# A planned order: the offsets of its due times put in a table with three phases

## The chip, the cores and the metric

One core of one Trainium2 chip. The time is that of the device for one execution, in microseconds (us). The core has TensorE (PE) for matmuls, VectorE (DVE), ScalarE (ACT) and GpSimd (POOL) for elementwise work, and SyncE (SP), which issues most of the DMAs. Each engine works through a queue of its own that is written when the kernel is built.

## The reference

Attention with random features feeds a two-layer network. 8 batches, 8 heads, 576 positions, head size 64, 128 features; the network has 4608 tokens, width 512, inner width 2048. All of it is float32.

```python
def phi(x):                                   # x is q or k, scaled by D ** -0.25
    h = einsum('bhsd,md->bhsm', x, omega) - sum(x * x) / 2
    return exp(h - max(h)) / sqrt(m)
kv = einsum('bhsm,bhsd->bhmd', phi(k), v)
z = sum(phi(k), axis=2)
x = einsum('bhsm,bhmd->bhsd', phi(q), kv) / (einsum('bhsm,bhm->bhs', phi(q), z) + 1e-6)
h = x.transpose(0, 2, 1, 3).reshape(4608, 512) @ w_in
out = (maximum(h, 0) + log1p(exp(-abs(h)))) @ w_out
```

## The kernel before

**Precision.** The layers' products are made of three matmuls each on operands split into a high part in a fast format and a rest: high x high, high x rest, rest x high. This is why every matmul line of a layer comes in threes (L923 to L925 for layer 1, written to `h`; L952 to L954 for layer 2, written to `acc`). The weights come as 64-bit words and are turned into such pairs in the first part of the kernel (`plan_weights`, lines L274 to L303).

**Attention.** Four heads of a batch are a quad; there are two quads in each of the 8 batches. A unit is one or two position tiles of keys or of queries of a quad (`plan_unit`). It loads a tile `xk` or `xq`, takes squares and norms, projects it, takes maxima over the features and the exponent. Keys and the first batches' queries are projected in one pass (`project`, L399); queries of later batches and some tails are split first (`spq`, L413 and L417) and projected with `product` (L424). A key tile gives its buffer back with its second maxima, a split tile with its norms. Key units are added up for z (`add`) and, when all five tiles are there, multiplied with v in a `burst` (L563, L664). Queries are divided by the denominators (`den`, L785), transposed on DVE (`flip`, L816), sent to DRAM and back in another order (`away`, L823; `back`, L839), and multiplied with kv (`num` in `plan_x`, L865). The result, split into high and rest, is the input of the layers. It lies in a ring of 1024 tokens.

**Layers.** Ten blocks of tokens (two of 256, then eight of 512) with 16 steps of the inner width each (`plan_step`): twelve matmuls of layer 1, three activations for the softplus on ACT, `plus`, `high` and `low` (the rest of the softplus, L946), then three matmuls of layer 2 for each 128 tokens. After 16 steps a block is copied out and stored.

**The order.** Nothing in it is a loop at run time. All work is first put down as `Work` items with a cost on each engine that may take it, a due time, what must be done before, and the buffers it takes and gives. `in_order` then plays the whole kernel through: it finds the engine on which the earliest item could start, takes of that engine's items that could start within `PATIENCE` of it the one with the lowest due time (less `GLUE` for half-array matmul groups behind another such group), and moves that engine's clock on by the item's cost. Items due more than `AHEAD` after the earliest unfinished one are left out. The outcome is one sequence, from which every engine's queue is written. At run time the queues hold to it, with semaphores where one needs the other. Costs are formulas: a load of n bytes is `max(0.55, n / 360e3)` us on SP, and its data count as there `DL` = 2.3 us later.

A due time is a base time plus an offset. The bases come from the place of the unit or step (`FIRST`, `NEXT`, `PACE` = 2.92 us for a step, `SPREAD`); the offset was a number written in each call, one for each kind of work:

```python
ld = do(
    "SP", dma(size), due - 2.45, load, behind=prev.get("load"),
    take=[("w" if early else "x", b, "x")], delay=DL, spare=2 if early else 0,
)
```

Of the buffers, there is one for the tiles of later batches (`"x": 1`), one for split tiles, three for features, two for `h`. Ahead of 70 us of the plan, `with_fill` puts filling matmuls (`fill`, L1104) where PE would have a gap.

Of the kernel before, what the change touches and what calls it, by code (L numbers as in the profile page):

```python
# [17 lines left out]
PSUM = bass.MemoryType.PSUM  # L18
# [3 lines left out]
D = 64  # L22
# [12 lines left out]
AHEAD = 211.97  # L35
MARGIN = 0.00
# [4 lines left out]
PATIENCE = {"PE": 0.00, "DVE": 0.00, "ACT": 0.17, "POOL": 0.00, "SP": 1.29}  # L41
LEAN = {"DVE": 0.22, "POOL": 0.14, "ACT": 0.00}
# [5 lines left out]
GLUE = 0.35  # L48
HOLD = 0.00
LATER = 4.74  # L50
EARLY_Q = 0.52
EARLY_T = 0.00

# [134 lines left out]
def favor_softplus_kernel(ctx, tc, q0, k0, qx, kx, tx, vv, om, wi, wo, out):  # L188
# [55 lines left out]
    def dma(size, n=1):  # L244
        return max(0.55 * n, size / 360e3)
# [19 lines left out]
    def plan_weights(nm, fc, due):  # L265

        src, w = (wi, w1) if nm == "i" else (wo, w2)
        last = fc == NFC - 1
# [33 lines left out]
        def low_part(e):  # L302
# [5 lines left out]
            "SP", 1.46, due + 8.41, load, delay=DL, spare=0 if last else 2,  # L308
# [3 lines left out]
        a = do(("ACT", "DVE"), (aw, dw2), due, low_bits, after=[l], port=True)  # L312
        b = do("ACT", aw, due, rebias, after=[l])
        c = do("DVE", dw, due, joined, after=[a, b], port=True)
        d = do(
            ("ACT", "DVE"), (aw, dw2), due, high_part, after=[c] + (in_w if last else []), take=[("w", box, "w")], port=True,
# [3 lines left out]
        return do(("DVE", "POOL"), (dw, pw), due, low_part, after=[d], give=[(box, "raw")], port=True)  # L320


    def plan_save(q, y, due, after):

        def save():
            c, t = slice(2 * q.qd, 2 * q.qd + 2), slice(q.b * D, (q.b + 1) * D)
            nc.sync.dma_start(rest[:, c, t], y["r"])

        saves.append(do("SP", 0.6, due, save, after=after, give=[(y, "rs")], delay=DL))
# [17 lines left out]
    def plan_unit(q, kind, us, due, early, other=None):  # L347

        u = us[0]
        nm = f"{kind}{q.nm}_{u}"  # L350
# [112 lines left out]
        def exponent(j):  # L463
# [9 lines left out]
            "SP", dma(size), due - 2.45, load, behind=prev.get("load"),  # L473
# [3 lines left out]
        s = do(("POOL", "ACT"), (pool(w), act(w)), due, squares, after=[ld])  # L477
# [3 lines left out]
        if q.b < SPLIT["t" if tail else kind]:  # L481
            r = do("DVE", dve(w), due + 18.07, norms, after=[s], behind=prev.get("norms"), take=sm)
            prev["norms"] = r
            p = do(
                "PE", 0.02 + 0.224 * nt, due - 25.82, project, after=[ld], mode="r",
# [9 lines left out]
            e = do("DVE", dve(n), due - 9.42, less_norms, after=[e], port=True)  # L495
            e = do("DVE", dve(n), due - 7.64, bias, after=[e], port=True)
            for j in range(2):
                give = [(b, ("ppb", j))]
                es.append(do(
                    "ACT", n // 2 * 0.25, due + 9.96, lambda j=j: exponent(j), after=[e], behind=es[0] if j else None,  # L500
                    give=give + ([(b, "sms")] if j else []),
                ))
        else:
            hs, ls, l = [], [], None
            for j in range(2):
                h = do(
                    ("ACT", "DVE"), (act(w) + 0.1, dve(w, 2) + 0.115), due + 0.00, lambda e, j=j: high(e, j), after=[ld], behind=hs[-1] if hs else None,
# [3 lines left out]
                l = do(("DVE", "POOL"), (dve(w) + 0.115, pool(w) + 0.05), due - 113.62, lambda e, j=j: low(e, j), after=[h], behind=l, port=True)  # L511
                ls.append(l)
            r = do("DVE", dve(w), due - 20.57, norms, after=[s] + ls, behind=prev.get("norms"), take=sm, give=[(b, "x")])
            prev["norms"] = r
            e, p = None, prev.get("product")
            for t in range(nt):
                p = do(
                    "PE", 0.236, due - 27.09, lambda t=t: product(t), after=ls, behind=p, take=[(kind_, b, ("ppb", t))],
# [3 lines left out]
                    ("ACT", "DVE"), (act(2 * M, PSUM), dve(2 * M)), due - 49.46, lambda e, t=t: first(e, t), after=[p], behind=e,  # L522
                    take=[] if t else phs,
                )
                e = do("DVE", dve(2 * M), due - 32.71, lambda t=t: second(t), after=[c], give=[(b, ("ppb", t))])
            prev["product"] = p
            e = do("DVE", dve(n * M) + 0.07 * (len(to) - 1), due + 72.38, all_maxima, after=[e, r])
            e = do("DVE", dve(n), due - 62.34, less_norms, after=[e], port=True)
            e = do("DVE", dve(n), due - 40.07, bias, after=[e], port=True)
            es = []  # L530
            for t in range(nt):
                es.append(do(
                    "ACT", 0.587, due - 48.11, lambda t=t: exponents(t), after=[e], behind=es[-1] if es else None,
# [15 lines left out]
    def plan_keys(q, us, due, b, es, early):  # L549
# [36 lines left out]
        def plan_turn(after, give=[]):  # L586
            old = quads[q.n - 2].nums if q.n >= 2 else []
            t = do("PE", 0.15, due - 17.12, turn, after=[after], take=[(any_, q.slots, "kv")], give=give)
            q.kvl = do(
                ("ACT", "DVE"), (act(2 * M, PSUM), dve(2 * M)), due - 5.81, turned, after=[t] + old,  # L590
# [4 lines left out]
        if early:  # L595
# [16 lines left out]
            def first_scaled():  # L612
# [4 lines left out]
                "PE", 0.97 if u < 4 else 0.5, due + 44.03, outer, after=es + [q.kvm], give=[(b, "x")],  # L617
                take=[("acc", q.slots, "kt")] if u == 0 else [],
            )
            if u == 4:  # L620
                q.kvl = do(
                    "ACT", act(4 * D + 4, PSUM), due - 27.00, first_scaled, after=[q.kvm], give=[(q.slots, "kt")],
# [4 lines left out]
        def add(e):  # L627
# [16 lines left out]
            ("POOL", "DVE"), (k * pool(w), k * dve(w)), due + 4.30, add, after=es + [q.sum],  # L644
# [29 lines left out]
        def in_z():  # L674
# [6 lines left out]
        ldv = do("SP", 1.8, due + 46.00, load_v, take=[("v", q.slots, "v")], delay=DL)  # L681
        q.kvm = do(
            "PE", 0.1 + 0.224 * 12, due - 54.75, burst, after=q.es + [ldv, q.sum], take=[(any_, q.slots, "kt")],
            give=[(x, "phs") for _, x in q.units] + [(q.slots, "v")], mode="c",
        )
        a = do("ACT", act(4 * M, PSUM), due + 43.95, lambda: scaled(4 * M), after=[q.kvm], give=[(q.slots, "kt")])
        t = plan_turn(a)
        r = do("SP", 0.55, due - 26.01, out_z, after=[a], delay=DL)
        q.zc = do(
            "SP", 0.73, due + 17.88, in_z, after=[r, t], take=[("zb", q.slots, "zb")], give=[(q.slots, "s")], delay=DL  # L690
        )

    def plan_first(q, u, due, b, es, nm):
# [51 lines left out]
        def x_low():  # L745
# [3 lines left out]
        t = do("PE", 0.13 * n, due - 142.98, turn, after=es, take=[("any", y, "tp")])  # L749
        h = do(("ACT", "DVE"), (act(n * M, PSUM), dve(n * M)), due - 126.19, turned, after=[t], give=[(y, "tp")])  # L750
        a = do(
            "PE", 0.9, due - 147.22, num, after=[h, q.kvl], take=[("any", y, "nb")], behind=q.nums[-1] if q.nums else None,
            give=[(q.slots, "zb")] if u == NU - 1 else [],
        )
        i = do("DVE", 0.25, due - 94.20, invert, after=[a], take=[("dn", y, "dns")], port=True)
        v = do("DVE", dve(4 * D), due - 35.90, divide, after=[i], give=[(y, "nb"), (y, "dns")])
        k = do("PE", 0.28, due - 15.07, back, after=[v], take=[("any", y, "xb")], give=[(b, "x")])
        q.nums.append(a)
        h = do(
            ("DVE", "ACT"), (dve(2 * w), act(2 * w, PSUM)), due + 25.84, x_high, after=[k], take=[("pt", y, "rs")] if u == 4 else [],  # L760
# [5 lines left out]
        l = do("DVE", dve(2 * w), due - 36.37, x_low, after=[h], give=[(y, "xb")])  # L766
# [3 lines left out]
    def plan_queries(q, u, due, bu, es, nm, first):  # L770
# [21 lines left out]
        def divide(e):  # L792
# [4 lines left out]
            "DVE", 1.7 if u < 4 else 1.3, due + 43.55, den, after=es + [q.zc], take=[("dn", b, "dns")],  # L797
            give=[(q.slots, "zb")] if u == NU - 1 else [], port=True,
        )
        d = do("DVE", 0.09, due - 60.76, invert, after=[d])  # L800
        return do(("POOL", "DVE"), (1.0 * f, dve(n * M)), due + 84.05, divide, after=[d], give=[(b, "dns")], port=True)
# [410 lines left out]
```

## Time and profile before

| | |
|---|---|
| three runs | 1013.47, 1015.00, 1015.49 us; median 1015.0 |
| span of the profiled execution | 1014.7 us |
| its mean granted TensorE clock | 0.998 |
| PE, PEld busy | 998.7, 808.7 us |
| DVE, ACT, POOL busy | 744.1, 659.4, 118.7 us |
| HBM | 85.68 MB read, 27.03 MB written |

The profile has no time of its own for the profiled execution beside its span; the span is 0.3 us under the median of the runs and inside their spread. PEld is the loading of weights into the array, which goes on beside the matmuls. Where a row says "idle before" or puts a wait in brackets, it names the engine and line that ended it.

### The profile page before, as it was taken

Reading aid. Unit: us, or ns where it says so; the run is one execution under the profiler, and the core shown is the slowest. Engines: PE = TensorE matmul, PEld = TensorE weight load, DVE = VectorE, ACT = ScalarE, POOL = GpSimd, SP = SyncE. Lnnn points to the kernel's source line nnn. Section 1 sums busy time; section 2 is a strip of 40 time slices with the busy share of each in tenths; the row PEclk is TensorE's granted clock in tenths of the full one; section 3 lists DMA queues with packets and bytes.
Section 4 is the critical chain, followed back from the end, with each engine's and each line's share of the span. In section 5 each row is a group of like instructions: output and inputs, shape, how many; then the busy total and the mean of one; then the engine's idle time right before and its main releaser. Section 6 shows DMA issues by size and latency. Waiting matters only on the chain.

```text
span 1014.7 us, 17024 instructions
## 1 busy us (share of the span) xinstructions
PE 998.7 (98%) x5752; PEld 808.7 (80%) x5752; DVE 744.1 (73%) x2027; ACT 659.4 (65%) x1592; POOL 118.7 (12%) x125
## 2 busy tenths in 40 slices
PE   9999999999999999999999999999999999999997
PEld 8788788877777787878787777778788778888886
DVE  6999988988888787878787887878797733223222
ACT  6999977766666675856576666656575644444443
POOL 2212221010021010110112011201011100000000
PEclk9999999999999999999999999999999999999999
DMA  9774354443442424343333433352433121001001
GB/s 350 300 274 165 115 151 126 151 114 94 125 141 69 139 80 145 115 130 94 118 127 102 113 96 111 95 146 73 138 129 89 42 79 63 1 1 42 1 1 42
DMA packets 64174, 113.81 MB, mean 112 GB/s; under 512 B 18236, under 2 KB 36824, under 8 KB 64088
## 3 DMA queue, kind: packets, MB, share of 16 engines
q1 hardware_dynamic: 63848, 112.34, 34.9%
q8 instruction: 46, 0.75, 0.3%
q10 hardware_dynamic: 240, 0.39, 0.1%
q14 instruction: 40, 0.33, 0.1%
HBM read 85.68 MB, written 27.03 MB: 111 GB/s over the span
## 4 chain that ended last, share of the span: by engine, by line
PE 80%; DMA 7%; DVE 6%; ACT 5%; issue 1%; SPq 0%; POOL 0%; DVEq 0%; POOLq 0%
PE acc L952 12%; PE h L923 12%; PE acc L953 11%; PE acc L954 11%; PE h L924 11%; PE h L925 11%; PE xp L865 3%; PE kt L563 2%; PE ppk L399 2%; PE ppq L424 2%; DMA xk<-kx 2%; DVE junk L785 2%; DMA xq<-q 1%; DMA xq<-qx 1%; DMA rawo<-wo 1%
## 5 line engine op out<-in xcount | busy, mean ns | idle before, releaser
L923 PE MATMUL h<-xh,wi 128*128 128x512 f32 (+1 forms) x640 | 239.6, 374 | 1.5 <-DVE u L938 1.4
L924 PE MATMUL h<-xl,wi 128*128 128x512 f32 (+1 forms) x640 | 236.0, 369 | 0.0
L925 PE MATMUL h<-xh,wi 128*128 128x512 f32 (+1 forms) x640 | 235.5, 368 | 0.0
L952 PE MATMUL acc<-wo,gh 128*128 128x512 f32 x576 | 231.1, 401 | 0.5 <-ACT kvs L581 0.5
L953 PE MATMUL acc<-wo,gh 128*128 128x512 f32 x576 | 225.4, 391 | 0.0
L954 PE MATMUL acc<-wo,gl 128*128 128x512 f32 x576 | 224.8, 390 | 0.0
L929 ACT ACTIVATE u<-h 128x512 f32<-128x512 f32 (+1 forms) x160 | 89.1, 558 | 168.8 <-PE h L925 161.6
L938 DVE SCALAR_TENSOR_TENSOR u<-h,u 128x512 f32<-128x512 f32 (+1 forms) x160 | 101.3, 633 | 119.4 <-ACT u L935 117.2
L923 PEld LDWEIGHTS h<-xh,wi 128*128 128x128 f32 x640 | 120.5, 188 | 30.0 <-issue 5.4
L925 PEld LDWEIGHTS h<-xh,wi 128*128 128x128 f32 x640 | 120.5, 188 | 20.5
L924 PEld LDWEIGHTS h<-xl,wi 128*128 128x128 f32 x640 | 120.6, 188 | 18.8
L952 PEld LDWEIGHTS acc<-wo,gh 128*128 128x128 f32 x576 | 108.1, 188 | 30.0 <-issue 7.2
L954 PEld LDWEIGHTS acc<-wo,gl 128*128 128x128 f32 x576 | 108.2, 188 | 24.0 <-DVE gl L946 0.4
L953 PEld LDWEIGHTS acc<-wo,gh 128*128 128x128 f32 x576 | 108.4, 188 | 17.9
L942 ACT CAST gh<-u 128x512 fp32r<-128x512 f32 (+1 forms) x122 | 71.4, 585 | 57.0 <-PE acc L953 56.0
L946 DVE TENSOR_TENSOR gl<-u,gh 128x512 fp32r<-128x512 f32 (+1 forms) x128 | 86.1, 673 | 27.8 <-ACT gh L942 25.9
L935 ACT ACTIVATE u<-u 128x512 f32<-128x512 f32 (+1 forms) x160 | 94.4, 590 | 4.8
L932 ACT ACTIVATE u<-u 128x512 f32<-128x512 f32 (+1 forms) x160 | 94.5, 591 | 3.9
L785 DVE CUSTOM_DVE_ANT_0 junk<-phq,zb 128x128 bf16<-128x128 f32 (+1 forms) x228 | 78.1, 342 | 17.3 <-ACT phq L446 1.4
L794 POOL TENSOR_TENSOR phq<-phq,dnq 128x512 f32<-128x512 f32 (+1 forms) x43 | 45.5, 1063 | 212.1 <-DVE dnq L790 114.2
L946 POOL TENSOR_TENSOR gl<-u,gh 128x512 fp32r<-128x512 f32 (+1 forms) x32 | 36.2, 1131 | 280.3 <-ACT gh L942 147.5
L469 ACT ACTIVATE phk<-ppk,smk 128x128 f32<-128x128 f32 x230 | 63.6, 376 | 3.5 <-DVE smk L461 2.1
(129 smaller groups left out, 1293.6 us busy)
## 6 DMA issues: line engine op xcount, KB each, us to landing
xk<-kx SPq DMA_DIRECT2D x28, 512.0 KB
xq<-qx SPq DMA_DIRECT2D x28, 512.0 KB
fdq<-flq SPq DMA_DIRECT2D x28, 512.0 KB
qq<-fdq SPq DMA_DIRECT2D x112, 128.0 KB
rawi<-wi SPq DMA_DIRECT2D x16, 512.0 KB
rawo<-wo SPq DMA_DIRECT2D x16, 512.0 KB
out<-o SPq DMA_DIRECT2D x32, 256.0 KB
v<-vv SPq DMA_DIRECT2D x14, 576.0 KB
```

The source lines that it names most:

```text
L785: nc.vector.tensor_tensor_reduce(jk[r, c % jk.shape[1]], ph[r, c], q.zb[r, h], 1.0, 1e-6, ALU.mult, ALU.add, dn[r, 0, c : c + 1])
L923: nc.tensor.matmul(b["h"], wh, xh[:, cc, t], start=cc == 0, stop=False)
L924: nc.tensor.matmul(b["h"], wh, xl[:, cc, t], start=False, stop=False)
L925: nc.tensor.matmul(b["h"], wl, xh[:, cc, t], start=False, stop=cc == NCC - 1)
L929: nc.scalar.activation(b["u"], b["h"], AF.Abs)
L932: nc.scalar.activation(b["u"], b["u"], AF.Exp, scale=-1.0)
L935: nc.scalar.activation(b["u"], b["u"], AF.Ln, bias=1.0)
L938: nc.vector.scalar_tensor_tensor(b["u"], b["h"], 0.0, b["u"], ALU.max, ALU.add)
L946: (nc.vector if e == "DVE" else nc.gpsimd).tensor_tensor(b["gl"], b["u"], b["gh"].bitcast(F32), ALU.subtract)
L952: nc.tensor.matmul(acc[tt], gh, w2[fc][:, 0], start=fc == 0, stop=False)
L953: nc.tensor.matmul(acc[tt], gh, w2[fc][:, 1], start=False, stop=False)
L954: nc.tensor.matmul(acc[tt], gl, w2[fc][:, 0], start=False, stop=fc == NFC - 1)
```

## The change

Every offset moves into a table, `DUE`, under the name of its kind of work, with three numbers: `by(key, due)` adds the one of the current phase. The phase is set on entry to three functions, from the weights' chunk, the unit's batch or the block. All but a few of the numbers in the table differ from those in the calls before. Besides, `AHEAD`, `GLUE` and some of `PATIENCE` and `LEAN` have other values. Costs, buffers, base times, the functions that emit instructions and `in_order` itself stay as they are.

```diff
-AHEAD = 211.97
+AHEAD = 223.0942
-PATIENCE = {"PE": 0.00, "DVE": 0.00, "ACT": 0.17, "POOL": 0.00, "SP": 1.29}
-LEAN = {"DVE": 0.22, "POOL": 0.14, "ACT": 0.00}
+PATIENCE = {"PE": 0.0164, "DVE": 0.00, "ACT": 0.1684, "POOL": 0.00, "SP": 1.1241}
+LEAN = {"DVE": 0.2277, "POOL": 0.0900, "ACT": 0.00}
-GLUE = 0.35
+GLUE = 0.9002
+PHASE = [0]
+def by(key, due):
+    return due + DUE[key][PHASE[0]]
+DUE = {
+    "weights.load": (9.28, -4.63, 1.37),
...
+    "weights.high_part": (-0.76, -4.04, -53.28),
...
+    "unit.load": (-1.26, -0.71, 5.53),
...
+    "unit.project": (-24.15, -41.49, -112.25),
+    "unit.maxima": (-2.46, -38.05, 0.88),
...
+    "unit.norms2": (-20.57, -20.57, -12.55),
+    "unit.product": (-27.09, -27.09, -98.56),
...
+    "unit.all_maxima": (72.38, 72.38, -55.22),
...
+    "queries.den": (43.55, 41.33, 97.91),
...
+    "flip.away": (-64.23, 73.34, -92.28),
...
+    "step.layer1": (39.90, -4.88, -5.74),
...
+    "step.low": (4.10, 86.96, -5.17),
+    "step.layer2": (62.69, 4.31, 4.11),
...
+    "step.store": (52.41, -38.32, 125.86),
...
+}
     def plan_weights(nm, fc, due):
+        PHASE[0] = 0 if fc < 5 else 1 if fc < 10 else 2
...
-            "SP", 1.46, due + 8.41, load, delay=DL, spare=0 if last else 2,
+            "SP", 1.46, by("weights.load", due), load, delay=DL, spare=0 if last else 2,
...
     def plan_unit(q, kind, us, due, early, other=None):
+        PHASE[0] = min(q.b, 2)
...
-            "SP", dma(size), due - 2.45, load, behind=prev.get("load"),
+            "SP", dma(size), by("unit.load", due), load, behind=prev.get("load"),
...
-                    "DVE", dve(n // 2 * M), due - 5.19, lambda j=j: maxima(j), after=[p, e], give=[(b, "x")] if j and not early else [],
+                    "DVE", dve(n // 2 * M), by("unit.maxima", due), lambda j=j: maxima(j), after=[p, e], give=[(b, "x")] if j and not early else [],
...
     def plan_step(i, t0, n, fc, due, acc, box):
+        PHASE[0] = 0 if i < 2 else 1 if i < 4 else 2
...
-                "PE", 0.70 if n < TB else 1.36, due, lambda ccs=ccs: layer1(ccs), after=[x for cc, x in need if cc in ccs] + [done_w["i", fc]], behind=a,
+                "PE", 0.70 if n < TB else 1.36, by("step.layer1", due), lambda ccs=ccs: layer1(ccs), after=[x for cc, x in need if cc in ccs] + [done_w["i", fc]], behind=a,
...
-        l = do(("DVE", "POOL"), (dve(n), pool(n)), due + 8.00, low, after=[h], give=[(b, "us")], port=True)
+        l = do(("DVE", "POOL"), (dve(n), pool(n)), by("step.low", due), low, after=[h], give=[(b, "us")], port=True)
```

The other calls change in the same way.

## Rows read from the trace of the kernel before

**Rows 1.** The page's first part: busy time, share of the span, instructions.
```profile
PE 998.7 (98%) x5752; PEld 808.7 (80%) x5752; DVE 744.1 (73%) x2027; ACT 659.4 (65%) x1592; POOL 118.7 (12%) x125
```

**Rows 2.** Windows: start and end us, length, busy us (instructions) by engine, clock, DMA.
```profile
0.00:54.00 54.00, 50.67 (x430) 43.77 (x430) 45.91 (x169) 44.81 (x127) 12.61 (x21) 1.00 0.80 305
54.00:120.00 66.00, 62.86 (x467) 52.58 (x468) 63.09 (x178) 62.27 (x171) 13.05 (x13) 1.00 0.59 202
120.00:800.00 680.00, 676.24 (x3933) 541.11 (x3932) 566.94 (x1562) 455.20 (x1131) 91.94 (x91) 1.00 0.38 114
900.00:1000.00 100.00, 100.00 (x443) 82.84 (x442) 26.52 (x40) 47.52 (x79) 0.00 (x0) 1.00 0.03 11
```

**Rows 3.** Waits of PE: line, releaser, us in total, times, longest.
```profile
PE ppq L424 <- DVE spq L417: 2.6, 3, 1.2
PE ppk L399 <- DMA xk<-kx: 2.3, 3, 1.1
```

**Rows 4.** Timeline of PE at four places: start us, duration us, instruction, idle before.
```profile
72.27 0.28 PE L924 MATMUL h<-xl,wi 128*128 128x256 f32 x1
72.39 0.28 PE L925 MATMUL h<-xh,wi 128*128 128x256 f32 x1
73.77 1.16 PE L399 MATMUL ppk<-omf,xk 64*128 64x128 f32 x16 [1.10 <-DMA xk<-kx]
...
234.22 0.39 PE L925 MATMUL h<-xh,wi 128*128 128x512 f32 x1
235.63 1.16 PE L399 MATMUL ppk<-omf,xk 64*128 64x128 f32 x16 [1.02 <-DMA xk<-kx]
...
556.58 0.28 PE L424 MATMUL ppq<-omr,spq 128*128 128x256 f32 x1
558.04 0.61 PE L424 MATMUL ppq<-omr,spq 128*128 128x256 f32 x3 [1.18 <-DVE spq L417]
558.49 0.40 PE L923 MATMUL h<-xh,wi 128*128 128x512 f32 x1
...
668.02 0.35 PE L424 MATMUL ppq<-omr,spq 128*128 128x256 f32 x1
669.60 0.62 PE L424 MATMUL ppq<-omr,spq 128*128 128x256 f32 x3 [1.23 <-DVE spq L417]
```

**Rows 5.** Chain that ended last, around those places: start us, us, what.
```profile
67.38 6.35 DMA xk<-kx
...
230.06 5.44 DMA xk<-kx
...
547.52 1.25 DVE flq L816
548.78 0.33 SPq L823
...
549.29 5.40 DMA xq<-qx
...
661.07 5.19 DMA xq<-qx
```

**Rows 6.** Timeline of PE before its first long run.
```profile
52.70 1.16 PE L1104 MATMUL fill<-ident 128*128 128x128 f32 x8
54.54 0.39 PE L923 MATMUL h<-xh,wi 128*128 128x256 f32 x1 [0.69 <-DVE u L938]
```

**Rows 7.** Timeline of PE around one xp group.
```profile
343.58 0.39 PE L925 MATMUL h<-xh,wi 128*128 128x512 f32 x1
343.90 1.30 PE L865 MATMUL xp<-qq,kvs 128*64 128x320 f32 x8
345.13 0.50 PE L923 MATMUL h<-xh,wi 128*128 128x512 f32 x1
```

**Rows 8.** Timeline of PE at the end: its last matmul.
```profile
1008.57 0.39 PE L954 MATMUL acc<-wo,gl 128*128 128x512 f32 x1
```

**Rows 9.** Groups by line and shape, DVE: count, busy us, mean ns, idle before.
```profile
L946 DVE TENSOR_TENSOR gl<-u,gh 128x512 fp32r<-128x512 f32 x109 | 78.2, 717 | 27.1 <-ACT gh L942 25.5 <-issue 0.3
```

More of the change, by code (lines that the diff above doesn't have):

```diff
@@ L47 @@
 UW = 512
[L48 to L49 removed]
+GLUE = 0.9002
+HOLD = 0.0000
 LATER = 4.74
@@ L476, in plan_unit @@
         prev["load"] = ld
-        s = do(("POOL", "ACT"), (pool(w), act(w)), due, squares, after=[ld])
+        s = do(("POOL", "ACT"), (pool(w), act(w)), by("unit.squares", due), squares, after=[ld])
         r, sm = None, [("sm", b, "sms")]
@@ L499, in plan_unit @@
                 es.append(do(
-                    "ACT", n // 2 * 0.25, due + 9.96, lambda j=j: exponent(j), after=[e], behind=es[0] if j else None,
+                    "ACT", n // 2 * 0.25, by("unit.exponent", due), lambda j=j: exponent(j), after=[e], behind=es[0] if j else None,
                     give=give + ([(b, "sms")] if j else []),
@@ L506, in plan_unit @@
                 h = do(
-                    ("ACT", "DVE"), (act(w) + 0.1, dve(w, 2) + 0.115), due + 0.00, lambda e, j=j: high(e, j), after=[ld], behind=hs[-1] if hs else None,
+                    ("ACT", "DVE"), (act(w) + 0.1, dve(w, 2) + 0.115), by("unit.high", due), lambda e, j=j: high(e, j), after=[ld], behind=hs[-1] if hs else None,
                     take=[] if j else [("sp", b, "sps")], port=True,
@@ L517, in plan_unit @@
                 p = do(
-                    "PE", 0.236, due - 27.09, lambda t=t: product(t), after=ls, behind=p, take=[(kind_, b, ("ppb", t))],
+                    "PE", 0.236, by("unit.product", due), lambda t=t: product(t), after=ls, behind=p, take=[(kind_, b, ("ppb", t))],
                     give=[(b, "sps")] if t == nt - 1 else [],
@@ L532, in plan_unit @@
                 es.append(do(
-                    "ACT", 0.587, due - 48.11, lambda t=t: exponents(t), after=[e], behind=es[-1] if es else None,
+                    "ACT", 0.587, by("unit.exponents", due), lambda t=t: exponents(t), after=[e], behind=es[-1] if es else None,
                     give=[(b, "sms")] if t == nt - 1 else [],
@@ L765, in plan_first @@
             return
-        l = do("DVE", dve(2 * w), due - 36.37, x_low, after=[h], give=[(y, "xb")])
+        l = do("DVE", dve(2 * w), by("first.x_low", due), x_low, after=[h], give=[(y, "xb")])
         for p in range(2):
@@ L998, in store @@
                     e.dma_start(out[(2 * u + j + 1) * S - D : (2 * u + j + 1) * S, :], o["t"][j * D : (j + 1) * D])
-            a = do("DVE", 0.34, due - 27.47, left, after=[ends[tt]], take=[("end" if last else "t2", o, "s")])
-            r = do("ACT", 0.27, due - 57.46, right, after=[a], give=[(box, ("acc", i, tt))])
-            do("SP", 0.75 if t0 < B * MAIN else 1.5, due + 38.64, store, after=[a, r], give=[(o, "s")], delay=2.0)
+            a = do("DVE", 0.34, by("step.left", due), left, after=[ends[tt]], take=[("end" if last else "t2", o, "s")])
+            r = do("ACT", 0.27, by("step.right", due), right, after=[a], give=[(box, ("acc", i, tt))])
+            do("SP", 0.75 if t0 < B * MAIN else 1.5, by("step.store", due), store, after=[a, r], give=[(o, "s")], delay=2.0)
     def plan_rest(due):
@@ L1014, in load @@
                 nc.sync.dma_start(b["t"], rest[:, 2 * i : 2 * i + 2])
-            l = do("SP", 2.0, due, load, after=saves, take=[("x", b, "x")], delay=4.0)
+            l = do("SP", 2.0, by("rest.load", due), load, after=saves, take=[("x", b, "x")], delay=4.0)
             for p in range(2):
```

156 lines of the change are left out of this document (104 added, 52 removed).

## The prediction

> **What bounds the kernel now.** I read the engine totals first, then the stretches, then TensorE's waits, then the chain behind each long wait. The totals say 98% busy for TensorE (PE) against 73% for DVE and 65% for ACT [rows 1]. A busy PE in this profile is not a PE at its peak, so the stretches have to bear it out. Between 900 and 1000 us only the two-layer network runs: 443 matmuls in 100 us, 225.7 ns each, with no idle time at all [rows 2]. Between 120 and 800 us PE is busy for 676.24 of 680 us although attention is mixed in, while DVE has 113 us to spare [rows 2]. So PE sets the end, and an order can win only what PE loses. It loses in four places: ahead of 54 us 3.3 us without work (54.00 - 50.67), between 54 and 120 us 3.1 us, between 120 and 800 us 3.8 us [rows 2], and behind its last matmul the output's way out.
>
> The Trainium skill (Perfetto Trace Analysis, Identifying the Most-Contended Engine) says that TensorE's headroom is not to be judged by matmul busy time but by the share of time in which it loads weights. Taken at its word on the whole span, 808.7 us of 1014.7 [rows 1], it would leave 206 us of headroom. The trace limits that: in the stretch without one wait, the weight loads take 82.84 of 100 us [rows 2], so here 83% is full, and 808.7 / 0.828 = 976 us would be the span of a PE that never stood. That is 38 us of room at the very most, and it includes the start, the tail and the changes of tile mode.
>
> Named waits of PE that matter: for split queries (spq) three, 2.6 us; for the key tile's load (xk) three, 2.3 us [rows 3]. The wait as the profile gives it is shorter than what it costs, since a matmul's duration overlaps the next; the price is the distance of two starts less the normal step. That step is 0.23 us for 512 columns [rows 2] and 0.12 us for 256 (72.27 to 72.39). Four places stand out [rows 4]: 72.39 to 73.77 (1.38 - 0.12 = 1.26 us), 234.22 to 235.63 (1.41 - 0.23 = 1.18), 556.58 to 558.04 (1.46 - 0.12 = 1.34) and 668.02 to 669.60 (1.58 - 0.12 = 1.46). Sum: 5.24 us.
>
> Behind each of the four the chain shows a load of the one x buffer: 6.35, 5.44, 5.40 and 5.19 us long [rows 5]. The planner counts on less: `dma(size)` of a 512 KB tile is 524288/360000 = 1.46 us, and DL = 2.3 us behind it makes 3.76. It is short by 1.4 to 2.6 us at each of the four, as much as PE then stands or more. The planned order puts the matmul where its operand should have landed, and on the chip everything behind that matmul in PE's queue stands with it: the layer work behind the products of 556.58 starts at 558.49 [rows 4]. At 556 the load itself sat in SP's queue behind the issue for the turned queries, which waited for DVE's transpose (1.25 us at 547.52) [rows 5].
>
> **The change part by part.** No instruction's kind, shape or count is touched: the functions that emit work are the same, only the number added to each due time differs. So nothing is added to PE's matmuls; only the few filling matmuls ahead of 70 us and the choice between two engines can differ. What moves is the order in all five queues, SP's loads among them.
>
> *Loads against the matmuls that need them.* For batches from the third on, the load of a unit goes from -2.45 to +5.53, its projection from -25.82 to -112.25, its products from -27.09 to -98.56. A matmul with so early a due time goes as soon as the plan thinks its operand is there, in both kernels: the operand decides, not the number. The planned arrival is still 3.76 us behind the issue, for the costs are unchanged. Whether the matmul now lands behind the true arrival hangs on what else is ready, and an order that is good when durations are longer is one with other PE work in that place. Bounds: all four stalls go (-5.2), or they stay and each of the seven batches after the first gets one (three have one after 120 us, so four more, at 1.33 us, the mean of those three: +5.3). I take all four gone and one of the mean size (1.31) new: -5.2 + 1.3 = **-3.9 us**. I lean to the gain since each stall is a misfit of 1.2 to 1.5 us where a step of the layers that could stand before it is planned at 2.92 us (PACE).
>
> *The start.* At 52.70 eight filling matmuls are followed by 0.69 us of waiting for DVE; from the fill's start to the next real matmul (54.54) 1.84 us go [rows 6]. In the first phase the offsets hardly move for weights (load 8.41 to 9.28, high part 0 to -0.76) and units (projection -25.82 to -24.15), but layer 1 of the first two blocks goes to +39.90 and layer 2 from +10.23 to +62.69, so attention and weights go before them more often on DVE and ACT (DVE is busy 63.09 of the 66 us to 120, ACT 62.27 [rows 2]; that is why order there counts). Bounds: the 3.3 + 3.1 us of idle PE either go by two thirds (-4) or grow by as much (+4). I take half of the 1.84 us: **-0.9 us**.
>
> *DVE's order in the steady part.* With base times unchanged, the difference of two offsets says who is served first. The key maxima rose from -5.19 to +0.88 while the softplus remainder (`step.low`) fell from +8.00 to -5.17: the remainder gains 19 us on the maxima. The query maxima went the other way, +72.38 to -55.22, and the denominators from +43.55 to +97.91. DVE's spare 113 us in 680 hide this as a rule; where not, see the second rival. I take 0, bounds -2 and +8.
>
> *Changes of tile mode.* GLUE goes from 0.35 to 0.90, a bonus for two half-array groups that are both ready. A group of eight xp matmuls pays 343.90 - 343.58 - 0.23 = 0.09 us on the way in [rows 7] and by my estimate as much on the way out, and there are 28 of them (seven batches, two quads, two parts). Against due times tens of us apart, half a microsecond of bonus rarely decides. Bounds: ten pairs more or fewer, 10 x 0.2 = 2 us either way; I take 0.
>
> *The tail.* From the start of the last matmul (1008.57) to the end of the span 6.1 us go [rows 8]: its own run, half of the output tile on DVE, half on ACT, then the store. The change moves the stores' due times (38.64 to 125.86 at the end), but nothing else is left for SP by then. 0.
>
> Sum: 1014.7 - 3.9 - 0.9 = 1009.9 us in the time of the profiled execution. Its span is 0.3 us under the median of the runs, 1015.0, so **1010.2 us**.
>
> **The rivals.**
> (a) *Nothing net.* A queue that runs in order and a plan with the same short costs must misfit somewhere; removed stalls come back elsewhere. For it: the loads in the chain [rows 5] take 5.2 to 6.4 us, not the planned 3.8, and most loads of the kernel still don't reach PE; what hides them is the order, and all of it is dealt anew. Against: between 900 and 1000 us PE stands for nothing at all, so layer work is on hand to fill with, given the right place. 1014.7 + 0.3 = 1015, at most 2 either way.
> (b) *Slower: the x buffer is held longer.* There is one x buffer (`"x": 1`); a key tile frees it by its second maxima, which now rank behind the softplus remainder. One such remainder takes 0.72 us [rows 9]. The next load starts that much later. It decides from the point at which the tile lands later than its sixteen matmuls' place in PE's queue, which was so at 234 us already. If it holds for one load in each of the twelve quads from the third batch on, 12 x 0.72 = 8.6 us come on top: 1015 + 8.6 = 1023.6; for half of them 1019.3. Against it: the plan counts the buffer's release itself, and puts the matmul later.
> (c) *The start too.* If the new first phase also saves the larger part of the 6.4 us of idle PE ahead of 120 us (5 us) and no new stall comes up: 1015 - 5.2 - 5.0 = 1004.8, and 2 less with better pairing of the modes, 1002.8.
>
> **How the numbers follow.** Forecast 0.46, with its own range 1006 to 1013; nothing net 0.22; slower 0.14; the start too 0.18. Low end 1002 (below (c) with pairing), high end 1018 (half of (b) just left out). A measurement here can tell about 0.2%, 2 us. Faster by more than that, under 1013.0: 0.43 + 0.18 + 0.03 of (a) = 0.64. Within: 0.03 + 0.14 of (a) = 0.17. Slower: 0.14 + 0.05 of (a) = 0.19.
>
> **What would show it.** Right: in TensorE's waits those for spq and xk sink from 4.9 us to under 2, no distance of two starts over 1 us after 120 us, the last matmul starts near 1004. The start: the first layer-1 matmul of the long run before 54 us, or fewer fills ahead of it. (b): more and longer waits of PE for xk after 120 us, and SP's load waiting longer for key maxima. (a): as much idle PE as before, at other lines. The forecast is wrong if the last matmul starts later than 1007 us, or if the gain lies ahead of 54 us alone.

## The result and the profile after

The changed kernel takes 1021.45 us (median of six runs, 1019.68 to 1023.30) against 1014.98 (six runs, 1013.47 to 1015.81): ratio 1.0062, 95% interval 1.0047 to 1.0077. It is slower by some 6 us, or 0.6%, where 5 us less were forecast, and it lies outside the range. Of all executions told of below, one of the kernel e12 took 1646.11 us and stands in no ratio.

The page of the changed kernel, first part (busy us, share, instructions; compare [rows 1]):

```profile
PE 1002.8 (98%) x5752; PEld 808.5 (79%) x5752; DVE 744.2 (73%) x1982; ACT 665.9 (65%) x1616; POOL 142.6 (14%) x146
```

PE's work is the same, 5752 matmuls. POOL has 24 us more, in 21 more instructions. The windows over the same stretches (columns as in [rows 2]):

```profile
0.00:54.00 54.00, 50.64 (x427) 43.85 (x428) 45.23 (x169) 44.53 (x128) 12.39 (x20) 1.00 0.87 334
54.00:120.00 66.00, 64.05 (x480) 53.98 (x478) 64.44 (x178) 63.36 (x174) 15.01 (x15) 1.00 0.56 181
120.00:800.00 680.00, 674.87 (x3905) 535.87 (x3905) 569.99 (x1532) 459.84 (x1151) 114.63 (x111) 1.00 0.37 115
900.00:1000.00 100.00, 100.00 (x443) 82.81 (x442) 27.22 (x41) 47.18 (x79) 0.00 (x0) 1.00 0.03 11
```

The start is better (PE busy 64.05 us of 66 where it was 62.86), the steady part worse (674.87 where it was 676.24, with 28 matmuls fewer done), the pure layers exactly as before, and the granted clock is 1.00 in each. PE's waits (line, releaser, us in total, times, longest; compare [rows 3]):

```profile
PE h L1004 <- DVE u L1019: 1.5, 3, 0.7
PE ppq L504 <- DVE xl L965: 1.3, 1, 1.3
PE ppq L504 <- DVE spq L497: 1.2, 4, 0.5
...
PE ppq L504 <- ACT u L1016: 0.7, 1, 0.7
...
PE ppk L479 <- DMA xk<-kx: 0.4, 1, 0.4
```

The waits for the load of keys sank from 2.3 to 0.4 us and those for split queries from 2.6 to 1.2, under the forecast's bound of 2 us in sum; but new ones stand beside them, most ahead of split products (L504) or of layer 1. On the timeline of PE (start, duration, instruction, idle before) the worst three places, and then the last matmul, are these:

```profile
388.49 0.39 PE L1006 MATMUL h<-xh,wi 128*128 128x512 f32 x1
390.20 0.83 PE L504 MATMUL ppq<-omr,spq 128*128 128x256 f32 x4 [1.32 <-DVE xl L965]
...
446.45 0.39 PE L1035 MATMUL acc<-wo,gl 128*128 128x512 f32 x1
447.34 0.36 PE L504 MATMUL ppq<-omr,spq 128*128 128x256 f32 x1 [0.50 <-DVE spq L497]
447.97 0.62 PE L504 MATMUL ppq<-omr,spq 128*128 128x256 f32 x3 [0.27 <-DVE spq L497]
...
558.06 0.39 PE L1035 MATMUL acc<-wo,gl 128*128 128x512 f32 x1
559.19 0.36 PE L504 MATMUL ppq<-omr,spq 128*128 128x256 f32 x1 [0.74 <-ACT u L1016]
559.81 0.62 PE L504 MATMUL ppq<-omr,spq 128*128 128x256 f32 x3 [0.27 <-DVE spq L497]
...
1012.90 0.39 PE L1035 MATMUL acc<-wo,gl 128*128 128x512 f32 x1
```

By distances of two starts less the normal step, as in the prediction, these places cost 1.48, 0.66 + 0.51 and 0.90 + 0.51 us. Two distances are over 1 us (1.71 from 388.49, 1.13 from 558.06), where none after 120 us was forecast. The last matmul starts at 1012.90 where it was 1008.57 [rows 8]: 4.3 us later.

**The account of PE.** Summing the distance of every two starts less its normal step: up to 120 us PE loses 0.9 us less than before; from 120 to 800 us 5.2 more. Of these 5.2, places of 0.25 us and more make up 2.3 (6.9 us at eleven places, where there were 4.6 at five), and losses below 0.25 us each the other 2.9 (some 1.4 between split products, 1.1 at the first layer matmuls behind attention's). With the 0.9 saved at the start this makes the 4.3 us. The medians differ by more, 6.5 us. In the profiled executions of the other kernels, whose own time is known, it lies 1.7 to 2.3 us above the span. By this estimate before's profiled execution, of span 1014.7, was one of 1016.4 to 1017.0, slower than its median, while the changed kernel's, of 1020.62, was faster than its median.

### The profile page after: what moved, and what is told of

Read it like the earlier page. It is cut to its first block, busy times and chain, and to the rows that moved or that the text cites. A ratio compares the mean times of both kernels' runs of the same rounds, so it can differ in the third digit from the quotient of the medians.

```text
span 1018.8 us, 17056 instructions
## 1 busy us (share of the span) xinstructions
PE 1002.8 (98%) x5752; PEld 808.5 (79%) x5752; DVE 744.2 (73%) x1982; ACT 665.9 (65%) x1616; POOL 142.6 (14%) x146
## 4 chain that ended last, share of the span: by engine, by line
PE 82%; DVE 7%; ACT 6%; DMA 3%; issue 1%; SPq 0%; ACTq 0%; DVEq 0%
PE acc L1033 12%; PE h L1004 12%; PE acc L1034 11%; PE acc L1035 11%; PE h L1005 11%; PE h L1006 11%; PE ppk L479 3%; PE xp L945 3%; PE kt L643 3%; PE ppq L504 2%; DMA xq<-qx 2%; DVE spq L497 1%; ACT phk L549 1%; PE fill L1185 1%; PE kt L688 1%
## 5 line engine op out<-in xcount | busy, mean ns | idle before, releaser
L1023 ACT CAST gh<-u 128x512 fp32r<-128x512 f32 (+1 forms) x130 | 76.1, 585 | 49.5 <-PE acc L1034 48.0
L1027 DVE TENSOR_TENSOR gl<-u,gh 128x512 fp32r<-128x512 f32 (+1 forms) x119 | 77.9, 654 | 28.5 <-ACT gh L1023 27.1
L1027 POOL TENSOR_TENSOR gl<-u,gh 128x512 fp32r<-128x512 f32 (+1 forms) x41 | 48.3, 1178 | 240.3 <-ACT gh L1023 159.5
L526 ACT ACTIVATE phq<-phq,smq 128x128 f32<-128x128 f32 x194 | 60.6, 394 | 6.3 <-DVE smq L541 6.2
```

Of the source, the lines that this page charges most:

```text
L1027: (nc.vector if e == "DVE" else nc.gpsimd).tensor_tensor(b["gl"], b["u"], b["gh"].bitcast(F32), ALU.subtract)
```

## Where the new waits come from

The chain that ended last, that is, the work followed back from the end through what each step waited for, around those three places of the changed kernel (start us, us, what):

```profile
378.92 5.89 DMA xq<-qx
...
385.73 1.68 DVE spq L497
...
387.43 1.67 DVE spq L497
...
438.72 6.86 DMA xq<-qx
...
549.88 6.44 DMA xq<-qx
...
556.35 1.52 DVE spq L493
```

Two things stand in it at these three places. The first is a slow load. The medians from issue to landing, the sixth part of the changed kernel's page, are (names, engine, operation, count, KB, us):

```profile
xk<-kx SPq DMA_DIRECT2D x28, 512.0 KB, 3.5
xq<-qx SPq DMA_DIRECT2D x28, 512.0 KB, 4.4
...
v<-vv SPq DMA_DIRECT2D x14, 576.0 KB, 5.6
```

The trace tells the landing of only eight loads of xk and xq, so the first two medians stand on two and six loads. The first reader tells more where it waited for the load. Of the loads after 200 us whose end is known by either, the eight issued within 4 us behind a load of v took 4.1 to 6.9 us in the changed kernel and the other twelve 3.5 to 4.3; in the kernel before, four took 4.8 to 5.4 and the other thirteen 2.6 to 5.4, with a median of 3.65.

SP's queue in the changed kernel shows what was issued ahead of the one at 549.88, which needs 6.44 us:

```profile
548.96 0.33 SPq L903 DMA_DIRECT2D fdq<-flq  x1
549.41 0.36 SPq L732 DMA_DIRECT2D v<-vv  x1
549.88 0.71 SPq L456 DMA_DIRECT2D xq<-qx  x1
```

A load of v (576 KB) and the turned queries are issued 0.5 and 0.9 us ahead of it. While the loads of 378.9, 438.7 and 549.9 were under way, the DMA engines were busy 0.74, 0.95 and 0.83 of the time, against 0.37 between 120 and 800 us. In the kernel before, the load at 549.29 [rows 5] followed a load of v by 2.7 us; the one at 230.06 stood 11 us behind one, so v is not the whole story. The v loaded here is first read at 600.5 us; nothing asks for it at 549.

The second is DVE beside POOL. The two remainders of the split queries (L497) take 0.69 us by the median, but 1.68 and 1.67 us at 385.73 and 387.43; at 556.35 the first high part (L493) takes 1.52 us where the next one takes 0.43. POOL beside the two remainders, changed kernel:

```profile
385.43 1.42 POOL L1027 TENSOR_TENSOR gl<-u,gh 128x512 fp32r<-128x512 f32 x1 [7.39 <-ACT gh L1023]
386.82 1.73 POOL L713 TENSOR_TENSOR s<-phk 128x512 f32<-128x512 f32 x1
```

The first remainder ends 0.56 us after the POOL instruction it started beside, and the second as long after the next one. The matmul at 390.20 itself waited last for `xl` (L965, 1.32 us), which follows both remainders and `u` in DVE's queue and frees the bank that its product takes. The kernel before had such a remainder too, at a place which the prediction laid on the load alone. Its chain, and POOL beside it:

```profile
555.62 0.69 DVE spq L417
556.32 0.02 issue
556.34 1.66 DVE spq L417
```

```profile
556.02 1.42 POOL L946 TENSOR_TENSOR gl<-u,gh 128x512 fp32r<-128x512 f32 x1 [10.48 <-ACT gh L942]
```

Of the 1.34 us lost at 556.58 [rows 4] about 0.97 is this lengthening. In either trace (before and changed) every DVE instruction that takes more than 1.3 times the median of its kind lies beside a POOL instruction; the excess sums to 26.2 us (43 instructions) before and 45.4 us (69) after. The planner knows of it: POOL's work and DVE's work marked `port=True` exclude each other in the plan. But nothing makes the engines keep to the plan's times; they met 43 and 69 times after all. The Trainium skill (SBUF — State Buffer, Who interferes with whom) says that DVE instructions with two SBUF inputs, and copies and casts in some modes, wait out a POOL instruction that reads SBUF, while reductions never do. The trace agrees: the lengthened kinds are those, and no reduction is among them.

The other places are smaller, 2.9 us in sum, and not all of this kind: the chain goes back to a store of 4.36 us at 186 us, to ACT's copy of an output tile at 304, and to DVE's transposes (1.16 and 1.14 us) at 359 and 773.

## The experiments

The ratios are to runs of the kernel before on the same chip; they differ by up to 0.1% from the quotient of the two medians (e9: 1.0012 by medians), so that 1 us is hardly told apart here. The last matmul is that of the profiled execution. "Order" means the sequence from which all five queues are written.

| kernel | us | ratio (95%) | last matmul, us |
|---|---|---|---|
| e8, changed kernel again | 1021.15 | 1.0056 (1.0043 to 1.0069) | 1012.82 |
| e1, changed, key sums to DVE | 1020.49 | 1.0052 (1.0039 to 1.0064) | 1015.06 |
| e2, changed, remainders to DVE | 1020.37 | 1.0043 (1.0030 to 1.0057) | 1013.09 |
| e5, changed, v apart | 1018.34 | 1.0027 (1.0016 to 1.0038) | 1008.58 |
| e9, changed, v apart, both to DVE | 1017.04 | 1.0021 (1.0011 to 1.0030) | 1010.36 |
| e11, changed, v apart, before's choice | 1022.35 | 1.0071 (1.0059 to 1.0084) | 1015.12 |
| e14, changed, dealt anew | 1021.34 | 1.0060 (1.0044 to 1.0077) | 1013.55 |
| e15, changed, dealt anew | 1018.40 | 1.0035 (1.0021 to 1.0049) | 1011.64 |
| e17, changed, products back | 1019.90 | 1.0044 (1.0029 to 1.0059) | 1012.18 |
| e16, changed, 38 numbers back | 1017.48 | 1.0024 (1.0012 to 1.0036) | 1008.97 |
| e3, before, key sums to POOL | 1016.84 | 1.0012 (1.0000 to 1.0023) | 1008.51 |
| e4, before, remainders to DVE | 1015.64 | 1.0001 (0.9993 to 1.0010) | 1008.83 |
| e6, before, v apart | 1013.35 | 0.9976 (0.9966 to 0.9985) | 1005.52 |
| e7, before, other v closer | 1015.10 | 0.9991 (0.9978 to 1.0003) | 1007.68 |
| e10, before, v apart, remainders to DVE | 1012.97 | 0.9977 (0.9968 to 0.9986) | 1004.34 |
| e12, before, dealt anew | 1016.23 | 1.0012 (0.9998 to 1.0026) | 1008.28 |
| e13, before, dealt anew | 1012.54 | 0.9976 (0.9966 to 0.9986) | 1003.97 |
| e18, e13 with v apart | 1013.31 | 0.9975 (0.9965 to 0.9986) | 1004.63 |

**The changed kernel again (e8).** Nothing is edited.

> The changed kernel itself beside the other three on one chip, to have its time and a second profile of it: 1021 us, and the same places of stall if the order makes them.

Slower again, with stalls at the same places (186, 304, 359, 388, 446, 558, 773 us) and one new one, 0.47 us at 555. Most waits belong to the order, not to an execution.

**POOL's share (e1 to e4).** The order is kept; after planning, some works change their engine:

```diff
-        for w in with_fill(*in_order(works, room, AHEAD, MARGIN), room["any"], 70, fill):
+        out_, held = in_order(works, room, AHEAD, MARGIN)
+        for w in out_:
+            if w.engine == "POOL" and w.emit.__name__ == "add":   # e1: 15 sums; e2 and e4: 27 and 19 remainders `low` of 512 tokens
+                w.engine = "DVE"                                  # e3: the same 15 sums, DVE to POOL
+        for w in with_fill(out_, held, room["any"], 70, fill):
```

> The changed kernel, its order kept; the 15 key sums (add) that it gives to POOL go to DVE at the same places in the order. Sharing theory (some DVE instructions stand while POOL works, and the changed kernel gives POOL 24 us more): the 8 us by which DVE instructions are longer beside those sums go, POOL falls from 143 to about 121 us, the products that stood behind them at 388, 558, 668 us come on time, 1018.5 us (1017 to 1019.5). Order theory (the new places of the products in PE's queue alone cost the time): 1021.4 within 1 us, or slower, since DVE gets 11 us more to do.

> The changed kernel, its order kept; the 27 softplus remainders (low) of the 512-token blocks that it gives to POOL go to DVE. Sharing theory: 18 us of longer DVE instructions lie beside remainders on POOL; with them gone 1018 us (1016.5 to 1019.5), POOL at about 107 us. Order theory: 1021.4 within 1 us or slower by the 16 us that DVE gets on top.

> The kernel before, its order kept; the same 15 key sums that the changed kernel gives to POOL go to POOL here too (3 others are there already). Sharing theory: POOL at about 138 us, some 8 us more of longer DVE instructions, 1017.5 us (1016 to 1019). Order theory: 1015 within 1 us, since PE's queue is the same.

> The kernel before, its order kept; the 19 softplus remainders of the 512-token blocks on POOL go to DVE. Sharing theory: the two stalls of the split-query products at 556 and 668 us (1.34 and 1.46 us), where a DVE instruction took 1.65 us instead of 0.69 beside such a remainder, shrink to 0.4 each: 1013 us (1012 to 1014). Late-load theory of the prediction (these products wait since the load takes 5.4 us instead of 3.8): the stalls stay, 1015 within 1 us.

The lengthening on DVE follows POOL: 45.4 us in the changed kernel, 37.8 in e1, 29.3 in e2. The time hardly does, and the 1018 to 1018.5 us that the sharing theory asked of e1 and e2 were missed by some 2. Against 1.0056 to 1.0062, e1 gains about 0.4 to 1 us and e2 1.2 to 1.9, with intervals that overlap; e3 costs the kernel before 1.2 us (interval 0 to 2.3); e4 gains it nothing, though the stall at 556 sinks to 0.5 us. The stall at 668, which was expected to shrink as well, stays in e4: its remainders take 0.70 and 0.69 us again, but its load took 6.89 us, and PE loses 1.17 + 0.51 us. e4's chain there:

```profile
659.82 6.89 DMA xq<-qx
...
667.63 0.70 DVE spq L417
668.33 0.02 issue
668.35 0.69 DVE spq L417
```

A work taken off POOL lies on DVE instead. That most lengthened instructions hold up nobody is the likely reading, not a shown one.

**Loads of v away from the x loads (e5 to e7).** Only SP's queue is altered: a load of v less than 5 us ahead of an x load goes behind the second following x load (ten in the changed kernel, five in the kernel before). In e7 the other five of the kernel before go the opposite way, to 0.5 us ahead of an x load.

```diff
+def v_loads(out, close, since=200):
...
+        nxt = [at[y] for y in x if at[y] > at[w]]
+        if close and nxt[0] - at[w] >= 5:
+            key[w] = nxt[0] - 0.5
+        if not close and len(nxt) > 1 and nxt[0] - at[w] < 5:
+            key[w] = nxt[1] + 3.9
```

> The changed kernel, all queues as they are but for ten loads of v (from 200 us on) in SP's: each stood 2 to 4 us ahead of an x load and now stands behind the second x load that follows, some 14 us later; v is not needed for another 30 us. Shared-DMA theory: the x load behind a v load of 576 KB takes 5.9 to 6.9 us instead of some 4, and the products of the split queries stand for it; with v out of the way they come 1.5 to 2 us earlier at up to ten places, of which those at 304, 388, 446, 558 and 773 us show as stalls: 1017.5 us (1016 to 1019). Port theory (POOL alone) and order theory: 1021.4 within 1 us.

> The kernel before, only the five v loads that stand less than 5 us ahead of an x load moved behind the second x load that follows. Shared-DMA theory: the stalls at 234, 556 and 668 us lose the 1.2 to 1.6 us by which their loads were late, 1012.5 us (1011.5 to 1014). Port theory: 1015 within 1 us.

> The kernel before, only the five v loads that stand well apart moved, to 0.5 us ahead of the next x load: now ten of them stand there, as in the changed kernel. Shared-DMA theory: up to five new late loads, 1 us each, 1018.5 us (1017 to 1021). Port theory: 1015 within 1 us.

Both kernels gain about the same: the changed one some 3 us (1.0056 to 1.0027), the kernel before 2.4 us, which makes e6 faster than both kernels; by the last matmul it is 4.3 and 3.0 us. So the slow loads are a real cost and one cause of the waits in each kernel, but explain at most about 1 us of the difference between them. In e6 the stalls at 234 and 556 us are gone; two lines of its PE timeline at the first, to be held against [rows 4]:

```profile
233.99 0.39 PE L944 MATMUL h<-xh,wi 128*128 128x512 f32 x1
234.31 1.16 PE L418 MATMUL ppk<-omf,xk 64*128 64x128 f32 x16
```

The third stall that was expected to go, 668 in the kernel before, stands in e6 at 665 us with 1.46 us, for there a remainder still lies beside POOL. e6's chain:

```profile
657.98 5.26 DMA xq<-qx
...
664.17 0.70 DVE spq L436
664.86 0.02 issue
664.88 1.65 DVE spq L436
```

In e5 PE gains more than the time: its last matmul starts at 1008.58, 4.3 us earlier than in the changed kernel, but the end gives 1.6 us back. Its timeline behind the last matmul:

```profile
1009.15 2.87 ACTq L1098 DMA_DIRECT2D out<-o  x1
1012.14 0.37 ACT L1089 COPY o<-acc 128x256 f32<-128x256 f32 x1 [2.64 <-DMA out<-o]
```

The last copy on ACT waits 2.64 us for a store, and the span ends 7.5 us behind the last matmul's start instead of 5.9. e7 shows no effect, where up to five new late loads were expected. Four of the five moved loads have their first reader 7.05 us after their issue and the fifth 7.89, and those four readers start as late in the kernel before when its loads stand apart: a load that lands later there meets nobody.

**Both together (e9, e10), and the engines of before in the changed order (e11).** e9 is e5 with e1's and e2's edits, e10 is e6 with e4's. e11 is e5 with 121 works given the engine that they have in the kernel before:

```diff
+        for i in (59, 161, 185,
...
+            works[i].engine = "DVE"
+        for i in (77, 503, 513,
...
+            works[i].engine = "POOL"
+        out_ = v_loads(out_, False)
```

> The changed kernel with its v loads apart (1018.3 us) and besides all key sums and the softplus remainders of the 512-token blocks on DVE. If what is left over the kernel before (3 us at the last matmul) comes from POOL's work beside DVE's: DVE's lengthening falls from 45 to about 22 us and the time to 1016 us or less. If it comes from the order of the queues: 1018 within 1 us, as DVE gets some 27 us more of its own.

> The kernel before with five v loads apart (1013.35 us) and besides the 19 softplus remainders of the 512-token blocks on DVE. With v apart one stall over 1 us is left after 120 us: at 665 us 1.46 us, where the split query stood beside a remainder on POOL. If that goes and DVE has room for the remainders: 1012 us (1011 to 1013). If DVE has not: 1013.5 to 1015.

> The changed kernel with its v loads apart and its order kept, but each of the 121 works that the two kernels give to different ones of DVE and POOL goes where the kernel before has it (POOL at 119 us again). If the choice of engine is what is left of the loss: 1015.5 to 1016.5. If it is the order: 1018.3, or slower, as the choice doesn't fit the order.

e10 has no wait of PE left after 120 us that the profile names, and its longest remainder of split queries takes 818 ns (lines of that tile, duration min/median/max; the first is of the changed kernel):

```profile
L497 DVE TENSOR_TENSOR spq<-xq,spq x48: 684/687/1668, 175.3 to 775.9; 64x512 fp32r<-64x512 f32 x48
```

```profile
L436 DVE TENSOR_TENSOR spq<-xq,spq x50: 286/687/818, 176.3 to 784.2; 64x512 fp32r<-64x512 f32 x48, 64x128 fp32r<-64x128 f32 x2
```

At 667 us, where e4 lost 1.7 us and e6 1.46, e10 loses 0.29: that stall had two causes, and it took both edits to remove it. But its time is that of e6. e9 is at most 1 us better than e5, with intervals that overlap; its last matmul starts later (1010.36). e11 is slower by 4 us than e5: this choice of engines doesn't fit this order. With loads and POOL both out of the way the changed order is still 4.1 us behind the kernel before so treated (1017.04 and 1012.97).

**Other orders with the same planned end (e12 to e15).** One to three offsets are moved a little, and the planner is run again:

```diff
-("ACT", "DVE"), (act(w) + 0.1, dve(w, 2) + 0.115), due + 0.00, ...
+("ACT", "DVE"), (act(w) + 0.1, dve(w, 2) + 0.115), due - 0.27, ...   # e12
-            e = do("DVE", dve(n), due - 62.34, less_norms, after=[e], port=True)
+            e = do("DVE", dve(n), due - 81.03, less_norms, after=[e], port=True)   # e13
-            "DVE", dve(n * M), due - 5.32, flip, ...
+            "DVE", dve(n * M), due - 15.79, flip, ...   # e13
-    "step.layer1": (39.90, -4.88, -5.74),
+    "step.layer1": (35.27, -5.47, -3.56),   # e14
-    "step.layer2": (62.69, 4.31, 4.11),
+    "step.layer2": (66.54, 0.97, 7.88),   # e15
```

> The kernel before with one offset changed by 0.27 us (the weights' high part, 0.00 to -0.27); costs, bases and all other offsets stay. From that first difference on the planned order comes out otherwise (of 4282 works about half stand in the same place), with its planned end the same to 0.2 us. Eight of the ten v loads after 200 us then stand less than 5 us ahead of an x load, where five did. Theory A (the changed table's offsets have a fault of their own): this is the kernel before, 1015.6, at most 1 us either way. Theory B (the planner can't tell such orders apart and the chip can, by several us; before is a favourable draw): slower by 2 to 6 us, 1018 to 1021, with new stalls of PE over 0.5 us at other places than before's. By the v loads alone, at 0.5 us each of three more (2.3 us for five): 1017.

> The kernel before with two offsets changed (the taking off of the norms from -62.34 to -81.03, the flip of the turned queries from -5.32 to -15.79), planned end 0.5 us later. All ten v loads after 200 us stand about 2 us ahead of an x load. Theory A: 1015.6 to 1016.5. Theory B: 1018 to 1021, with the x loads behind the v loads at 5 to 7 us in the chain. By the v loads alone, five more at 0.46 us: 1018.

> The changed kernel with the three offsets of layer 1's step moved by 0.6 to 4.6 us, planned end the same to 0.1 us. Theory A: the fault of the changed table stays, 1020.5 to 1021.5. Theory B: somewhere between 1016 and 1023; a time outside 1020 to 1022 speaks for B.

> The changed kernel with the three offsets of layer 2's step moved by 3 to 4 us, planned end 0.6 us later. Theory A: 1020.5 to 1022. Theory B: somewhere between 1016 and 1023; a time outside 1020 to 1022.5 speaks for B.

Neither theory holds as it stands. Orders that the planner holds equal to within 1 us (by their own plans all six end between 994.8 and 995.7 us, the changed kernel 0.4 us ahead of the kernel before) lie 9 us apart on the chip, and e13 with 2.4 us less than before speaks against before being merely a lucky deal. Yet all three orders of the old offsets beat all three of the table. e13's window of the steady part:

```profile
120.00:800.00 680.00, 679.81 (x3946) 543.31 (x3945) 556.63 (x1570) 463.30 (x1121) 98.00 (x105) 1.00 0.36 114
```

PE stands 0.2 us in 680, and the last matmul starts at 1003.97. All ten of e13's loads of v are planned about 2 us ahead of an x load; the by-the-loads forecast of 1018 was wrong. SP's queue in e13 at one such place:

```profile
613.43 0.39 SPq L652 DMA_DIRECT2D v<-vv  x1
614.31 0.35 SPq L376 DMA_DIRECT2D xk<-kx  x1
```

That tile's first reader starts 5.66 us after its issue, late like the others, and still PE waits for nothing: in this order its queue asks for the tile's results late enough.

**Parts of the table (e16, e17), and e13 with v apart (e18).** e17 sets back one number, e16 38 of the third column's 66, those with which the planner's end stays within 0.4 us:

```diff
-    "unit.product": (-27.09, -27.09, -98.56),
+    "unit.product": (-27.09, -27.09, -27.09),   # e17
```

> The changed kernel with 38 of the 66 numbers of the third phase set back to the offsets of before (those that the planner bears, its end 0.4 us later); the first two phases and the other constants stay. If the loss sits in these numbers of the steady phase: 1013 to 1016.5. If it goes with what is left of the table (or the first phases): 1019 to 1022. If only the luck of the deal counts: anywhere from 1012 to 1022.

> The changed kernel with one number set back: the split products' third offset, -98.56 to -27.09, as before; planned end the same. The order differs from some 200 us on. If the early products are the fault (they stand in PE's queue as soon as the plan thinks their operand is there, and stall PE when the load is late): the stalls at split products go, 1016 to 1018. If not: 1018 to 1022, as the other deals of this table.

> The re-dealt kernel of e13 (1012.5, no wait of PE over 0.3 us after 120 us) with its ten v loads moved behind the second following x load. If an x load beside a v load costs only where PE's queue has no slack: no gain, 1012 to 1013. If it costs always, some 0.4 us each: 1008.5. If the v loads at their new place push aside others: 1013 to 1015.

e16 falls between its first two forecasts: it takes off about 3.5 us of the 6, its last matmul at 1008.97 and PE's losses from 120 us on at 4.7 us in large places, as in the kernel before. But it is a new deal too, its third forecast (anywhere from 1012 to 1022) holds as well, and e15 took off 2 to 3 us with three numbers of one step. POOL still has 138.1 us in it, so POOL's larger share can't be the cause by itself; the lengthening on DVE, though, is down to 24.9 us there. e17 takes off 1 to 2 us and its stalls only change places. e18 gains nothing, as expected if moving a load helps only where a matmul waits for it.

## Why the prediction was wrong

**The step that failed** is "Loads against the matmuls that need them": "I take all four gone and one of the mean size (1.31) new: -5.2 + 1.3". Three of the four went. The one at 556.58 stayed: the same load, the 41st of xk and xq in either kernel, is issued at 549.88 instead of 549.29, and its products lose 1.41 us where they lost 1.34. And instead of one new stall of 1.31 us, eleven places after 120 us lose 6.9 us in all (this one among them), and the losses too small to list grew by 2.9 us, which the step had no term for. It took a new order to be a repaired old one. The runs e12 to e15 show what it is: another deal, whose large losses range from 0.5 us (e13) to 7.4 us (e14).

**Its reason was half right.** The planned 3.76 us for a load are not short as a rule: the median of those thirteen known loads of the kernel before that stand apart from v is 3.65 us. They are short beside a load of v (4.1 to 6.9 us). And at 556 and 668 us it was not the load alone: the remainder beside POOL took 1.66 and 1.65 us instead of 0.69. That "a step of the layers that could stand before it" can hide the misfit is true (e13 shows it), but the changed order isn't such an order. Of the three offsets read in that step, the one of the loads doesn't decide it: with that third number set back alone the planner writes the same order, work for work (so it does with that of the remainders, `step.low`, or of the loads of v). The products' number does alter the order, and setting it back (e17) left 4.5 us of the loss; the projection's alters it too and was not timed.

**The start** came out at its number by luck: -0.9 us forecast, 0.9 us measured up to 120 us. But the saving is the stall at 72.39 us (1.26 us), which the prediction had booked under the loads. Of the 1.84 us of [rows 6], half of which was to go, 1.53 are left (here 53.41 to 54.94), and ahead of 54 us PE loses no less than before.

**DVE's order and the choice of engines.** DVE was costed at 0, by its spare time. The sum was right: its busy time stayed the same. What the step lacked was a term for POOL: it got 21 instructions more (`LEAN` for POOL, 0.14 to 0.09, is in the diff, but which number gave them wasn't isolated), and DVE 19 us more lengthening. By e1 and e2 that is worth at most 1 to 2 us of the loss.

**Tile modes and tail** were 0 and stayed near it: `GLUE` set back alone gives the same order in both kernels, and the end behind the last matmul went from 6.1 to 5.9 us. The losses at the first layer matmul behind a group of attention's, most of these half-array groups, rose by about 1 us (82 slow ones instead of 72 after 120 us, 0.107 us each).

**From span to time** the prediction added 0.3 us. By the 1.7 to 2.3 us of the other executions that was too little by some 1.5 us, whatever the change did.

**The rivals.** (a), "removed stalls come back elsewhere", was the right mechanism, but its bound of 2 us either way had nothing behind it. (b) has no support: PE waits less for keys, not more (0.4 us instead of 2.3), and its lever, the remainder's number, alters no order by itself. (c) did not come up.

**What stays open.** Setting back the third column's 38 numbers took off some 3.5 of the 6 us (e16), POOL's share and single numbers 1 to 2. As each such run is a deal of its own, it isn't shown that these numbers carry the loss. Nor is it shown why all orders of the table tried here lie above all those of the old offsets. With three of each that may still be chance.

## What to carry to other kernels

A planned order isn't better because a replay says so: here two plans 0.4 us apart came out 6 us the other way. A replay would have to lengthen what the chip lengthens, here loads beside other loads and two-input DVE work beside POOL; whether that makes it a better judge wasn't tried. When a change re-deals all queues of a kernel that is 98% busy, count on a scatter of several us (9 here), and don't price the new order by the old one's stalls. Deal several orders with the same planned end and time them: of the three from the old offsets the best was 2.4 us faster than the kernel before, for two numbers moved.

## What was not expected of the hardware

An x load of 512 KB issued 0.5 to 2.7 us behind one of 576 KB landed after 5.40, 5.89, 6.44 and 6.86 us in the places above, where loads that stand apart from v took 3.65 by the median. It isn't so always: in e13 tiles issued 2.4 us behind one had their first reader after 3.6 to 3.8 us. A remainder of 64x512 beside POOL takes up to 1.67 us instead of 0.69, and two in a row may both be hit. And a store issue on ACT's queue took 2.87 us once (e5), where the same line in the changed kernel took 0.57 us.
